# Filling TensorE's waits with f32 products, and eight row transfers for four, in a one-core decode block

## The chip, the cores and the metric

The kernel runs on one core of a Trainium2 chip. The time is the device time of one execution in microseconds (us). A profile is one execution of its own, recorded with every instruction and every DMA packet; its span runs from the first to the last instruction, and its own time is a little longer than the span.

## What is computed

One decode step for four sequences (B = 4, one token each, width D = 448), in f32: attention over a cache, and a pre-LayerNorm MLP behind it, both added to the row.

```python
B, Sq, D = 4, 1, 448
Hq, Hkv, Sk, Dh = 16, 8, 4096, 256
W = min(4096, max(256, Sk // 4))            # 1024: the last keys of the cache
q = (layernorm(x) @ wq).reshape(B, Sq, Hq, Dh).transpose(0, 2, 1, 3)
k, v = the last W of k_cache, v_cache       # two query heads share each of 8 kv heads
p = softmax(einsum("bhqd,bhkd->bhqk", q, k) * Dh ** -0.5)
h = x + einsum("bhqk,bhkd->bhqd", p, v).transpose(0, 2, 1, 3).reshape(B, Sq, Hq * Dh) @ wo
y = layernorm(layernorm(h))
return h + gelu(y @ w1 + b1) @ w2 + b2      # F = 1792
```

The keys and values of 8 groups are 64 MB, and with the weights the kernel reads some 88 MB once. Each matmul has few rows, since there are only four sequences and two heads to a group.

## The kernel before

**Groups.** The work goes over the 8 kv heads, called groups (`g`). Of each group the kernel needs: the part of wq (projection, L151), the keys (scores, L170), the softmax of 1024 scores (L182), the transposed probabilities `pT` (L202), the values (L215), and the part of wo (L233, L245), which adds into one PSUM tile `acc`.

**Loads.** The inputs are packed on the host so that a few large transfers bring them: `la`, `lb`, `lc`, `ld` (7 to 8 MB each, twice each) carry keys, values and weights in the order of use into a ring of three slots of SBUF (tiles `t`, `ta`, `tb`, `tc`, `td`, `te`; buffer numbers are left out in the profile). All of these are issued by SP (L57), in order; SP issues one when its slot is free. The last three slots are the `te`: e[0] has the keys of group 7 and w1, e[1] the values of group 6 and two parts of wo, e[2] the values of group 7 and w2, in pieces (L322 to L328; the last three pieces are 8, 4 and 2 parts of w2). Two small loads `wq_last` stand between the first keys and `ta` on SP's queue. ACT issues only the four transfers in question, the rows (L127): of each of the four quarters of a row, with 4 partitions of 704 numbers: x, b2 and b1 side by side, into tile `rs`, which POOL has cleared before. `rs` is read only at the end (`xb` in L386, `b2b` in L404, `b1b` in L429). Behind the row transfers ACT's queue has the table load and the copy of the first projection (L156).

**Engines.** TensorE's order is the order of the program text. The order on the other engines and the semaphores are set when the program is compiled. TensorE works on four column quadrants: a matmul of 32 output rows writes one quadrant, and four of them in a row go to four quadrants. An f32 matmul appears in the profile as two instructions.

**The last softmax.** For group 7 (`g + 1` with g = 6) the scores are followed by two matmuls on a bf16 tile of zeros, `idle`, into a PSUM tile that nobody reads (`warm0`), the transposes of p, ten more of the idle ones, and then the values of group 6, whose PSUM tile `po` takes the buffer of `warm0`:

```python
    keep_warm(2, warm0)
    transpose_p(g + 1, p)
    keep_warm(10, warm0)
    po = po_tile(g)
    values(g, vt, po)
```

Then come the values of group 7, the last parts of wo, the two LayerNorms, and the MLP: `pu` (w1, L416), `u` (gelu), `put`/`gT` (transposes), `pa` (the first 8 parts of w2, L449) with its copy `pas` on ACT (L453), `py` (the other 6 parts, L459, with `pas` added by L463), the result `res` (L465), and the output transfer.

Of the kernel before, what the change touches and what calls it, by code (L numbers as in the profile page):

```python
# [15 lines left out]
B, D = 4, 448  # L16
# [4 lines left out]
P = 128  # L21
# [4 lines left out]
FQ = F // 4  # L26
Q = 32
# [8 lines left out]
def block_kernel(ctx: ExitStack, tc, rows, wq0, k0, wq1, la, lb, lc, ld, k7, vo, w1, w2, out):  # L36
    nc = tc.nc
# [15 lines left out]
    def load(t, at, src, pieces=None):  # L53
        dst = t[:, at : at + src.shape[-1]]
        at = 0
        for n in pieces or (src.shape[-1],):
            nc.sync.dma_start(dst[:, at : at + n], src[:, at : at + n])  # L57
            at += n
        return dst

    def cut(t, sizes):
        parts, at = [], 0
        for n in sizes:
            parts.append(t[:, at : at + n])
            at += n
        return parts
# [11 lines left out]
    def keys(t):  # L78
        return t.rearrange("p (c b k) -> p c b k", c=2, b=B)
# [22 lines left out]
    yT = const.tile([P, ND + 1, Q], F32, name="yT")  # L102
# [21 lines left out]
    rs = const.tile([P, 2 * P + FQ], F32, name="rs")  # L124
    nc.gpsimd.memset(rs, 0.0)
    for j in range(4):
        nc.scalar.dma_start(rs[j * Q : j * Q + B, :], rows[j])  # L127
    xb, b2b, b1b = rs[:, :P], rs[:, P : 2 * P], rs[:, 2 * P :]


# [39 lines left out]
    def scores_half(g, h, kt):  # L170
        s = ps_s.tile([P, 512], F32, tag="s", name=f"s{g}_{h}")
        for c in range(2):
            for b in range(B):
                nc.tensor.matmul(  # L174
                    s[b * Q : (b + 1) * Q, :], qT[g % 2][:, c, b, :], kt[:, c, b, :],
                    start=(c == 0), stop=(c == 1),
                )
        m = work.tile([P, 1], F32, tag=f"mx{h}", name=f"mx{g}_{h}")
        nc.vector.reduce_max(m, s, axis=AX.X)  # L179
        return s, m  # L180

    def softmax(g, parts):  # L182
        halves, mx = zip(*parts)
        nm = work.tile([P, 1], F32, tag="nm", name=f"nm{g}")
        nc.vector.tensor_max(nm, mx[0], mx[1])
        nc.vector.tensor_scalar_mul(nm, nm, -SCALE)  # L186
        p = once.tile([P, 2 * 512], F32, tag="p", name=f"p{g}")
        sums = work.tile([P, 2], F32, tag="sums", name=f"sums{g}")
        for h in range(2):
            nc.scalar.activation(  # L190
                p[:, h * 512 : (h + 1) * 512], halves[h], AF.Exp, bias=nm, scale=SCALE,
                accum_out=sums[:, h : h + 1],
            )
        rec = work.tile([P, 1], F32, tag=f"rec{g % 3}", name=f"rec{g}")
        nc.vector.tensor_add(rec, sums[:, 0:1], sums[:, 1:2])
        nc.vector.reciprocal(rec, rec)
        return p, rec

    def scores(g, kt):
        return softmax(g, [scores_half(g, h, kt[h]) for h in range(2)])  # L200

    def transpose_p(g, p):  # L202
        for h in range(2):
            pt = ps_t.tile([P, 4, P], F32, tag="t", name=f"ppt{g}_{h}")
            for c in range(4):
                nc.tensor.transpose(pt[:, c, :], p[:, (4 * h + c) * P : (4 * h + c + 1) * P], ident)  # L206

            src = pt.rearrange("p (c i) (b q) -> p c i b q", i=2, b=B)
            for i in range(2):
                nc.vector.tensor_copy(  # L210
                    pT[g % 2][:, 2 * h : 2 * h + 2, :, i * REP : (i + 1) * REP], src[:, :, i, :, :REP]
                )
# [44 lines left out]
    def po_tile(g, pool=ps_o, tag="o"):  # L257
        return pool.tile([P, 2, DH], F32, tag=tag, name=f"po{g}")
# [22 lines left out]
    p, rec = scores(0, [keys(ka), keys(kb)])  # L281
# [7 lines left out]
    for g in (0, 3):  # L289
        ka, kb, wqt, va = cut(load(slot(f"ta{g}"), 0, la[g // 3]), (HALF, HALF, WEIGHTS, HALF))  # L290
        p, rec_next = scores(g + 1, [keys(ka), keys(kb)])
# [8 lines left out]
        p, rec_then = scores(g + 2, [keys(ka), keys(kb)])  # L300
# [11 lines left out]
        p, rec = softmax(g + 3, [first_half, scores_half(g + 3, 1, keys(kb))])  # L312
# [7 lines left out]
    g = HKV - 2  # L320
    e = [slot(f"te{i}") for i in range(3)]
    kt = [keys(t) for t in cut(load(e[0], 0, k7), (HALF, HALF))]  # L322
# [6 lines left out]
    p, rec_last = scores(g + 1, kt)  # L329


    warm0 = ps_o.tile([P, 512], F32, tag="o", name="warm0")

    def keep_warm(n, warm):
        for _ in range(n):
            nc.tensor.matmul(warm[:Q], idle[:, :Q], idle, start=True, stop=True)  # L336

    keep_warm(2, warm0)
    transpose_p(g + 1, p)
    keep_warm(10, warm0)  # L340
    po = po_tile(g)
    values(g, vt, po)
    po_last = po_tile(g + 1, ps_t, "t")
# [17 lines left out]
    for i in range(4):  # L361
        for j in range(4):
            nc.tensor.matmul(
                ph[j * Q : (j + 1) * Q], oT[(g + 1) % 2][:, i, :], columns(wo_last[:, i, :], j),
                start=False, stop=(i == 3),
# [3 lines left out]
    def w1_part(a, j):  # L369
        if a < 3:  # L370
            return slice(0, P), w1t[a][:, FQ * j : FQ * (j + 1)]
        rows = slice(H * (j // 2), H * (j // 2) + H)
        return rows, w1t[a][rows, FQ * (j % 2) : FQ * (j % 2 + 1)]
# [38 lines left out]
    for a in range(ND):  # L412
        m = Q if a == 0 else B
        for j in range(4):
            rows, w = w1_part(a, j)
# [31 lines left out]
    for c in range(first):  # L447
        j, m = c % 4, Q if c < 4 else B
# [6 lines left out]
    for c in range(first, NFC):  # L455
        for j in range(4):
            m, n = (Q, 2) if c == first else (B, 2 if j < 3 else 1)
# [80 lines left out]
```

## Time and profile before

| | |
|---|---|
| time, median of 3 runs | 215.27 us (214.98 to 215.72) |
| the profiled execution's own time | 214.81 us |
| its span | 213.0 us |
| mean granted TensorE clock in it | 0.848 |
| TensorE busy (matmul / weight load) | 137.4 us / 48.2 us |
| VectorE, ScalarE, GpSimd busy | 38.4, 21.2, 5.6 us |
| moved by DMA | 88.46 MB, mean 415 GB/s |

In the profile PE is TensorE, PEld its weight loads, DVE is VectorE, ACT is ScalarE, POOL is GpSimd and SP is SyncE; "SPq" and "ACTq" are their queues when they issue transfers. q1 is the DMA queue of SP, q10 that of ACT. Starts and lengths are in us from the span's start. A group of instructions is written as line, engine, operation, output<-input, shapes, count; brackets give the idle time before it and what ended it. For a transfer the last number is the median time from issue to landing.

### The profile page before, as it was taken

The numbers are of one execution on the slowest core, as the hardware profiler recorded it, in microseconds if no ns is written. First come the engines' busy times: TensorE is split into PE (matmuls) and PEld (weight loads), VectorE is DVE, ScalarE is ACT, GpSimd is POOL, SyncE is SP. The second block draws the span as 40 slices with busy tenths as digits, with TensorE's granted clock in tenths as the row PEclk, the third lists the DMA queues.
The fourth block names the chain that finished last, engine by engine and source line by source line (L and its number), as shares of the span: only waits on it lengthen the run. The fifth ranks groups of instructions, "written<-read, shape, count | busy, mean of one in ns | idle before, by whom it ended". The sixth has DMA issues, their size and how long they took to land.

```text
span 213.0 us, 2294 instructions
## 1 busy us (share of the span) xinstructions
PE 137.4 (64%) x971; PEld 48.2 (23%) x971; DVE 38.4 (18%) x167; ACT 21.2 (10%) x52; POOL 5.6 (3%) x17
## 2 busy tenths in 40 slices
PE   0456824872970595289398198239809876998993
PEld 0322211220220221023123022113202322334432
DVE  1420320320230012012114013100301223122320
ACT  0210110120020100021003001000000302000310
POOL 6100000000000000000000000000000000000110
PEclk9999995796697579769859959955965999999999
DMA  7999899999999999999999999999999998999990
GB/s 291 433 392 502 381 486 391 447 467 409 417 453 444 417 417 477 390 465 391 458 423 444 425 456 417 429 417 465 405 410 415 430 450 380 435 414 435 420 376 34
DMA packets 3289, 88.46 MB, mean 415 GB/s; under 512 B 384, under 2 KB 512, under 8 KB 1104
## 3 DMA queue, kind: packets, MB, share of 16 engines
q1 hardware_dynamic: 3248, 88.29, 96.7%
q8 instruction: 7, 0.11, 0.2%
q10 hardware_dynamic: 32, 0.05, 0.1%
q14 instruction: 2, 0.02, 0.0%
HBM read 88.26 MB, written 0.07 MB: 415 GB/s over the span
## 4 chain that ended last, share of the span: by engine, by line
DMA 64%; PE 29%; DVE 3%; ACT 1%; issue 1%; SPq 0%; ACTq 0%; DVEq 0%
DMA ta<-la 21%; DMA td<-ld 20%; DMA tb<-lb 16%; PE s L174 8%; DMA t<-k 8%; PE po L218 8%; PE ppt L206 2%; PE pu L416 2%; PE warm L336 1%; PE acc L247 1%; PE pq L154 1%; PE pot L239 1%; PE pa L449 1%; DVE o L235 1%; DVE mx L179 1%
## 5 line engine op out<-in xcount | busy, mean ns | idle before, releaser
L179 DVE TENSOR_REDUCE mx<-s 128x1 f32<-128x512 f32 x16 | 11.1, 691 | 61.0 <-PE s L174 61.0
L174 PE MATMUL s<-ta,qT 128*32 128x512 f32 x64 | 12.2, 935 | 8.9 <-DMA ta<-la 8.9
L156 ACT COPY qs<-pq 128x512 f32<-128x512 f32 x8 | 4.7, 585 | 112.3 <-PE pq L154 112.3
L190 ACT ACTIVATE p<-s,nm 128x512 f32<-128x512 f32 x16 | 10.9, 687 | 45.9 <-DVE nm L186 45.9
L174 PE MATMUL s<-td,qT 128*32 128x512 f32 x32 | 7.3, 1061 | 12.0 <-DMA td<-ld 12.0
L235 DVE TENSOR_SCALAR o<-po,rec 128x512 f32<-128x512 f32 x8 | 6.0, 751 | 47.1 <-PE po L218 47.1
L218 PE MATMUL po<-tb,pT 128*32 128x512 f32 x32 | 7.3, 1061 | 10.4 <-DMA tb<-lb 10.4
L154 PE MATMUL pq<-tc,yT 128*32 128x512 f32 (+1 forms) x20 | 3.9, 890 | 14.8 <-DMA tc<-lc 14.8
L206 PE MATMUL ppt<-ident,p 128*128 128x128 f32 x64 | 10.5, 286 | 2.0 <-ACT p L190 1.7
L218 PE MATMUL po<-tc,pT 128*32 128x512 f32 x64 | 10.5, 815 | 0.0
L160 PE MATMUL pqt<-ident,qs 128*128 128x128 f32 x32 | 6.6, 341 | 6.0 <-ACT qs L156 6.0
L174 PE MATMUL s<-tb,qT 128*32 128x512 f32 x64 | 9.1, 717 | 0.0
L206 PEld LDWEIGHTS ppt<-ident,p 128*128 128x128 f32 x64 | 6.7, 140 | 7.1 <-ACT p L190 7.1
L218 PE MATMUL po<-te,pT 128*32 128x512 f32 x64 | 7.9, 596 | 0.1
L162 DVE TENSOR_REDUCE sm<-pqt 128x16 f32<-128x64 f32 x8 | 1.8, 224 | 33.9 <-PE pqt L160 33.9
L174 PE MATMUL s<-t,qT 128*32 128x512 f32 x32 | 6.1, 925 | 2.6 <-DMA t<-k 2.6
L218 PE MATMUL po<-td,pT 128*32 128x512 f32 x64 | 7.3, 595 | 0.0
L336 PE MATMUL warm<-idle 128*32 128x512 bf16 x25 | 7.3, 382 | 0.0
L160 PEld LDWEIGHTS pqt<-ident,qs 128*128 128x128 f32 x32 | 4.2, 169 | 12.1 <-ACT qs L156 10.3
L174 PEld LDWEIGHTS s<-ta,qT 128*32 128x32 f32 x64 | 2.9, 163 | 17.4 <-issue 14.4
L239 PE MATMUL pot<-ident,o 128*128 128x128 f32 x32 | 5.2, 287 | 2.2 <-DVE o L235 2.2
L148 POOL TENSOR_TENSOR r<-ve_r,mhalf 128x1 f32<-128x1 f32 x2 | 1.1, 542 | 192.2 <-DVE ve_r L147 192.2
(129 smaller groups left out, 113.4 us busy)
## 6 DMA issues: line engine op xcount, KB each, us to landing
tc<-lc SPq DMA_DIRECT2D x2, 7936.0 KB
td<-ld SPq DMA_DIRECT2D x2, 7936.0 KB
ta<-la SPq DMA_DIRECT2D x2, 7040.0 KB, 29.4
tb<-lb SPq DMA_DIRECT2D x2, 7040.0 KB, 34.3
te<-vo SPq DMA_DIRECT2D x1, 4992.0 KB, 27.2
t<-k SPq DMA_DIRECT2D x1, 4864.0 KB, 16.4
te<-k SPq DMA_DIRECT2D x1, 4096.0 KB, 36.9
te<-w SPq DMA_DIRECT2D x2, 1792.0 KB, 28.0
```

The lines of the kernel that those rows point to most:

```text
L154: nc.tensor.matmul(pq[j * Q : (j + 1) * Q, cols], y, w, start=True, stop=True)
L156: nc.scalar.copy(qs, pq)
L160: nc.tensor.transpose(pt[:, i, :], qs[:, i * P : (i + 1) * P], ident)
L174: nc.tensor.matmul(s[b * Q : (b + 1) * Q, :], qT[g % 2][:, c, b, :], kt[:, c, b, :], start=(c == 0), stop=(c == 1),)
L179: nc.vector.reduce_max(m, s, axis=AX.X)
L190: nc.scalar.activation(p[:, h * 512 : (h + 1) * 512], halves[h], AF.Exp, bias=nm, scale=SCALE, accum_out=sums[:, h : h + 1],)
L206: nc.tensor.transpose(pt[:, c, :], p[:, (4 * h + c) * P : (4 * h + c + 1) * P], ident)
L218: nc.tensor.matmul(po[b * Q : (b + 1) * Q], pT[g % 2][:, c, b, :], vt[c][:, :, b, :], start=(c == 0), stop=(c == NKC // 2 - 1),)
L235: nc.vector.tensor_scalar_mul(o, po, rec)
L239: nc.tensor.transpose(pt[:, i, c], o[:, i, c * P : (c + 1) * P], ident)
L336: nc.tensor.matmul(warm[:Q], idle[:, :Q], idle, start=True, stop=True)
L416: nc.tensor.matmul(pu[j * Q : j * Q + m, :], zT[rows, a, :m], w, start=(a == 0), stop=(a == ND - 1),)
```

## The change

There are two edits. Around the last softmax, the twelve idle matmuls become three f32 products and two idle ones. A product multiplies yT with the first 512 columns of the last keys, which have landed by then; it writes the same unread tile. Two products stand ahead of the transposes of p, one product and the two idle matmuls behind them. And each of the four row transfers is split in two by columns: 256 numbers of x and b2, then 448 of b1, so that ACT issues eight.

```diff
     rs = const.tile([P, 2 * P + FQ], F32, name="rs")
     nc.gpsimd.memset(rs, 0.0)
     for j in range(4):
-        nc.scalar.dma_start(rs[j * Q : j * Q + B, :], rows[j])
+        parts = (slice(0, 2 * P), slice(2 * P, 2 * P + FQ))
+        for cols in parts:
+            nc.scalar.dma_start(rs[j * Q : j * Q + B, cols], rows[j][:, cols])
     xb, b2b, b1b = rs[:, :P], rs[:, P : 2 * P], rs[:, 2 * P :]
...
+    def fill(n):
+        for _ in range(n):
+            nc.tensor.matmul(warm0[:Q], yT[:, 0, :], kt[0][:, 0, 0, :], start=True, stop=True)
+
+    fill(2)
+    transpose_p(g + 1, p)
+    fill(1)
     keep_warm(2, warm0)
-    transpose_p(g + 1, p)
-    keep_warm(10, warm0)
     po = po_tile(g)
     values(g, vt, po)
```

## The prediction

> **What bounds the kernel now.** I read the page first, then the stages, then the waits of SP, the timeline of both ends, and the chain. The page's chain of what ended last:
>
> ```profile
> DMA 64%; PE 29%; DVE 3%; ACT 1%; issue 1%; SPq 0%; ACTq 0%; DVEq 0%
> ```
>
> Two thirds of the way to the end is transfers. The stages say how full they are (last two columns: DMA share of the 16 engines, GB/s; before them the granted TensorE clock):
>
> ```profile
> 2.00:206.00 204.00, 133.65 (x899) 46.44 (x899) 37.13 (x161) 20.35 (x49) 4.15 (x8) 0.84 1.00 430
> 207.00:208.00 1.00, 1.00 (x20) 0.30 (x16) 0.00 (x0) 0.00 (x0) 0.00 (x0) 1.00 0.60 240
> ```
>
> From 2 us to 206 the share is 1.00: the stream has no hole in which lost time could be made up, and it runs dry only within the last microseconds. A hole made anywhere arrives at the end whole. Two rows of the chain show the stream handing over to TensorE (start, length, what), here the first keys and the last ring slot:
>
> ```profile
> 1.18 16.36 DMA t<-k
> 117.86 42.28 DMA td<-ld
> 160.19 3.64 PE s L174 x16
> ```
>
> Keys 0 land at 17.54, ld's second load at 160.14, and TensorE starts on it at 160.19. From there it works without a DMA wait until the last weights. So two clocks meet at the end: TensorE's chain from 160.19, and the stream's last landing. Both edits touch one of them each.
>
> **Part one, the filling.** TensorE and ACT around the last softmax:
>
> ```profile
> 175.04 0.13 PEld L174 LDWEIGHTS s<-te,qT 128*32 128x32 f32 x4 [0.30 <-issue]
> 178.05 0.59 PE L336 MATMUL warm<-idle 128*32 128x512 bf16 x2
> 180.32 1.32 PE L206 MATMUL ppt<-ident,p 128*128 128x128 f32 x8 [1.68 <-ACT p L190]
> 181.57 2.33 PE L336 MATMUL warm<-idle 128*32 128x512 bf16 x10
> 183.96 0.16 PEld L218 LDWEIGHTS po<-te,pT 128*32 128x32 f32 x8 [0.55 <-PE warm L336]
> 183.97 4.50 PE L218 MATMUL po<-te,pT 128*32 128x512 f32 x40
> ```
>
> The ten idle ones behind the transposes are no filling of a wait: po's weight load waited 0.55 for them, nothing else. They cost 183.97 - 181.57 = 2.40 us on TensorE's chain. One idle matmul more costs (2.33 - 0.59)/8 = 0.217, and the last one of a group lasts 0.59 - 0.22 = 0.37.
>
> An f32 call makes two instructions (the eight calls of half the scores are the x16 above). The weight loads of a stage of full-length f32 products come in fours every 0.13 + 0.30 = 0.43 us, one for each column quadrant. The new products all write the same quadrant, which no row shows: between 0.11 each, if they overlapped as four quadrants do, and 0.43 each in series. I take 0.43, because the idle ones, which also share one quadrant, follow each other by their full 0.217.
>
> - Two products ahead of the transposes: 4 x 0.43 = 1.7, from 178.05 to 179.8. The transposes start at 180.32, when ACT has made p. Cost nothing; the cover is ACT and DVE's softmax, with 0.5 us to spare. Without that cover they would cost up to 1.7.
> - Behind the transposes: one product 0.86, one idle step 0.22, and the last one's 0.37: 181.57 + 1.45 = 183.02, against 183.90 before. The chain gains 0.88 (1.5 if the product overlapped, less than nothing only if TensorE ran at half clock, a rival below).
>
> Where that goes is read at the end:
>
> ```profile
> te<-vo SPq DMA_DIRECT2D x1, 4992.0 KB, 27.2
> 154.46 21.68 SPq L57 DMA_DIRECT2D te<-vo  x4
> te<-w SPq DMA_DIRECT2D x1, 896.0 KB, 26.1
> 207.83 0.64 PE L459 MATMUL py<-te,gT 128*32 128x128 f32 x16
> PEld py L459 <- DMA te<-w: 0.7, 1, 0.7
> 208.12 0.53 ACT L453 COPY pas<-pa 128x448 f32<-128x448 f32 x1 [1.56 <-PE pa L449]
> 208.70 0.43 PE L255 MATMUL py<-pas,sel 128*32 128x128 f32 x8 [0.23 <-ACT pas L453]
> 208.94 1.05 PE L459 MATMUL py<-te,gT 128*4 128x128 f32 x32
> ```
>
> vo's first load, issued at 154.46, lands 27.2 later at 181.7, ahead of the new 183.1, so values(6) is not held. The 896 KB of w2 are issued then (see the waits below) and land at 181.7 + 26.1 = 207.8: py starts at 207.83, right on the landing. A TensorE that comes 0.88 earlier waits there for the same landing. What remains is pas: its copy ends at 208.65, and adding its quadrants starts at 208.70. Earlier by 0.88, it no longer delays: sixteen py matmuls take about 0.45 (eight of the same shape and the step to the next take 0.24), so the next start is 208.28 and the gain 0.42. The last piece of w2, half as large (line 328), comes about 1.05 us behind at 430 GB/s, at 208.85, and is wanted at 208.28 + 0.24 + 0.45 = 208.97: just covered. **Part one is worth 0.4 us**, from 0 (covers gone) to 0.9 (if landings also moved).
>
> **Part two, eight transfers of the rows.** The four stand on ACT's queue; SP's at the same time, tb's load as the chain has it (issued, then 34.27 to landing), and what SP waited for (total, times, longest):
>
> ```profile
> 4.07 1.54 ACTq L127 DMA_DIRECT2D rs<-rows  x4
> 13.29 0.58 ACT L156 COPY qs<-pq 128x512 f32<-128x512 f32 x1 [6.37 <-PE pq L154]
> 1.63 1.55 SPq L267 DMA_DIRECT2D wq_last<-wq  x2
> 5.36 0.34 SPq L57 DMA_DIRECT2D ta<-la  x1
> 17.56 34.27 DMA tb<-lb
> SPq L57 <- DMA t<-wq: 2.2, 1, 2.2
> SPq L57 <- DMA t<-k: 11.9, 1, 11.9
> SPq L57 <- DMA te<-vo: 5.8, 2, 3.6
> ```
>
> Issuing four more costs ACT another 1.5 us at most, inside the 6.37 in which it waits for the first projection: nothing by itself. The waits are the point. ta waits for wq, and tb waits 11.9 us for the keys, to 17.56, though the third ring slot is still empty: neither needs the other's data. Count the transfers of SP and ACT together: wq, keys, four rows, two wq_last are eight; ta is the ninth and waited for the first, tb the tenth and waited for the second. At the end w2's last two pieces waited for vo: the 896 KB for its first load, eight before. So eight completion counters serve both queues in turn, and a transfer waits until the one eight before it has landed.
>
> With eight row transfers ta is the thirteenth and waits for the fifth. The kernel before hands the counters out in the order wq, keys, rows, wq_last. If that order stays, the fifth is the third row transfer; the two wq_last wait for the first and second row, ahead of ta on SP; the last row on ACT waits for the keys, and behind it stand ACT's table load and the copy of the first projection. When does the third row land? ACT's queue is q10; its packets in 8.8 to 11.5, 11.5 to 14.5, 14.5 to 16.3 and 16.3 to 17.5 (none earlier):
>
> ```profile
> q10 hardware_dynamic: 8, 0.01, 1.1%
> q10 hardware_dynamic: 8, 0.01, 1.0%
> q10 hardware_dynamic: 4, 0.01, 1.6%
> q10 hardware_dynamic: 12, 0.01, 2.8%
> ```
>
> Four transfers of four rows are 32 packets, eight each (four of data, four closing). They crawl between the large packets of the keys: the first is through by 11.5, the second by 14.5, the third only after 16.3, with the keys. Size does not set this pace, so halving the rows does not quicken it. ta is then issued not at 5.36 but at about 17.4 (17.6 if the keys themselves are what it waits for), with nothing behind the keys but crumbs. How long the engines stand still: the first bytes of the whole program, slices of 0.1 us from the start:
>
> ```profile
> DMA  0000000000000000099051046495593993996999
> 0.73 0.39 SPq L57 DMA_DIRECT2D t<-wq  x1
> t<-wq SPq DMA_DIRECT2D x1, 904.0 KB, 4.6
> t<-k SPq DMA_DIRECT2D x1, 4864.0 KB, 16.4
> ```
>
> Issued at 0.73, moving at 1.7: 1.0 from issue to bytes. ta moves from about 18.5. The engine that is last with the keys lost 18.5 - 17.54 = 1.0; the mean one, which at 430 GB/s is through with wq and keys (5.9 MB, 13.7 us from 1.7) and the small ones by about 16, loses 2.5. A load counts as landed with its last engine, and which one is last at the end may change, so the loss is an estimate between 1.0 and 2.5; I take 1.6, nearer the end that keeps the order of the engines. With no hole later it goes to the end whole, and 160.14 moves with 207.8, so part one stays worth 0.4.
>
> The Trainium skill, "DMA: Bandwidth & Descriptors", section Specifications, gives about 0.6 us to the first byte for transfers from SP or ACT; by it the loss would be 0.4 smaller and the sum 216.1. The row of this case says 1.0, and I keep it. The same page's Rules for kernel authors advise to coalesce small transfers, since under 64 KB one pays mostly overhead: the trace agrees with its 3 us from one row transfer (4 x 704 numbers) to the next.
>
> ACT's hold to 17.6 also delays what stands behind it:
>
> ```profile
> 17.68 6.06 PE L174 MATMUL s<-t,qT 128*32 128x512 f32 x32 [2.57 <-DMA t<-k]
> 24.64 0.33 SPq L57 DMA_DIRECT2D tc<-lc  x1
> ```
>
> Table load, copy, transposes and sums then follow the keys and move the first scores from 17.68 to about 21. That costs nothing: t's slot is handed to tc at 24.64 and would be at 28, while ta and tb keep the stream busy to 51.8 (17.56 + 34.27). Without that cover it would be 3.4.
>
> **Sum.** On the profiled execution, 214.81 with a span of 213.0: 214.81 + 1.6 - 0.4 = 216.0. It lay 0.46 under the median of 215.27, on which the forecast stands: 215.27 + 1.2 = 216.5.
>
> **Rivals.**
> 1. *ta is held longer*, 0.15. If seven rows stand ahead of the wq_last in the list, those wait for the keys, and ta for their issue (1.55): first bytes at 20.1, 1.5 later: 218.0. For it: the rows reach ACT late, behind a memset, at 4.07. Against it: wq_last's two issues came behind all four rows in the order of counters.
> 2. *ta is not held* (the other side: faster), 0.13. If the wq_last are listed ahead of the rows, or the added rows behind ta, ta waits for wq or for the first row, through by 11.5. It decides at about 15.5: issued before that, its bytes follow the keys without a hole. Then only the 0.4 is left: 214.9, and 214.4 if all of part one's 0.88 counts. Against it: the order of before, as above.
> 3. *The hole is small*, 0.1: the third row lands right behind its closing packets, which begin after 16.3. Issued at 16.6, ta moves at 17.6, a loss between 0.1 (last engine) and 1.6 (mean), say 0.6: 215.5.
> 4. *The filling overruns*, 0.04. At half clock (160 to 165 below, where sixteen score instructions take the 3.64 of the chain, 0.86 a round) 4 x 0.86 = 3.4 from 178.05 ends at 181.5, past 180.32: 1.2 late, the gain is gone, and the end is 0.3 late on top: 217.2. Against it:
>
> ```profile
> 160.00:165.00 5.00, 4.82 (x26) 1.35 (x26) 1.01 (x3) 0.00 (x0) 0.00 (x0) 0.50 0.97 416
> 178.00:180.00 2.00, 0.64 (x6) 0.10 (x1) 1.01 (x3) 0.51 (x1) 0.00 (x0) 1.00 1.04 444
> ```
>
> With TensorE busy 0.64 of 2 us the clock stayed at 1.00, and the change makes it busier there.
>
> **The numbers.** The forecast has 0.58, with its own range of 215.9 (loss 1.0) to 217.4 (loss 2.5). The range for 8 in 10 takes that, rival 3, the nearer part of rival 1 and the slower edge of rival 2: 214.9 to 217.8. A measurement of this kernel can tell 0.3%, 0.65 us, from no change: faster means under 214.6, slower over 215.9. Rival 2 centres just inside the first bound and reaches past it; I give 0.08 of its 0.13 to faster, since the 0.4 of part one can be up to 0.9. Its rest, rival 3 and a thin edge of the forecast are within: 0.2. The forecast's bulk and rivals 1 and 4 are slower: 0.72.
>
> **What would show it.** ta issued near 17.4 and not 5.36, with SP's wait before it on rows or keys; a hollow in the DMA share between 16.5 and 18.5; ld's second load landing near 161.7; ACT's first table load behind 17. At the end: fills done before p, values(6) about 0.9 us sooner after the transposes than the 2.40 of before, py again on the landing of w2 and no gap ahead of pas's quadrants. ta issued before 15 would make the prediction wrong in its sign.

## Result, and the profile after

The changed kernel takes 217.04 us (median of 6 executions, 216.85 to 217.24) against 215.5 for the kernel before in the same session (6 executions, 214.98 to 216.35): ratio 1.0071 (95% interval 1.0047 to 1.0094), slower by about 1.5 us. The profiled execution took 216.85 with a span of 215.1, at a mean granted clock of 0.849 (before: 214.81, 213.0 and 0.848). Lines of the changed kernel stand 2 further down than before's from line 129 on, and 7 further down behind the filling.

The start, in the timeline of after (start and length in us, queue or engine, line, operation):

```profile
4.07 13.50 ACTq L129 DMA_DIRECT2D rs<-rows  x8
10.77 3.78 SPq L269 DMA_DIRECT2D wq_last<-wq  x2
17.12 0.34 SPq L57 DMA_DIRECT2D ta<-la  x1
17.60 1.28 ACT L158 ACT_TABLE_LOAD   x1 [17.60 <-DMA rs<-rows]
21.31 5.36 PE L176 MATMUL s<-t,qT 128*32 128x512 f32 x32 [0.61 <-DVE qT L170]
27.59 0.33 SPq L57 DMA_DIRECT2D tc<-lc  x1
```

The eight row issues spread from 4.07 to 17.57, where four took 1.54. Behind them in the order of counters wq_last waits until 10.77 and ta until 17.12 instead of 5.36. What SP waited for (us in total, times, longest) names the rows, for wq_last and for the load of ta:

```profile
SPq L269 <- DMA rs<-rows: 11.4, 2, 9.2
SPq L57 <- DMA rs<-rows: 2.6, 1, 2.6
```

The hollow, in the stages (last two columns: DMA share and GB/s); first two rows from before, then two from after:

```profile
14.00:16.40 2.40, 1.08 (x4) 0.71 (x4) 0.48 (x3) 0.00 (x0) 0.00 (x0) 1.00 0.85 354
16.40:18.00 1.60, 0.32 (x4) 0.23 (x8) 0.00 (x0) 0.00 (x0) 0.00 (x0) 1.00 1.22 517
```

```profile
14.00:16.40 2.40, 0.00 (x0) 0.00 (x0) 0.00 (x0) 0.00 (x0) 0.00 (x0) 1.00 0.69 290
16.40:18.00 1.60, 0.00 (x0) 0.00 (x0) 0.00 (x0) 0.40 (x1) 0.00 (x0) 1.00 0.15 53
```

In these two stretches after has moved 64 x 2.4 + 464 x 1.6 = 896 thousand bytes less, or 0.9 MB (up to 14 us the two are level), which is 2.1 us at the mean rate of 430 GB/s. The chain of what ended last was 64% transfers and 29% TensorE; now the transfers have more of it, and it goes through the rows, then ta. The larger share comes with the filling and not with the rows: in the experiments below it is 79% with the filling alone and 63% with the rows alone. After's chain, and four pieces of it:

```profile
DMA 77%; PE 17%; POOL 1%; DVE 1%; ACT 1%; issue 1%; ACTq 0%; POOLq 0%
```

```profile
4.94 12.16 DMA rs<-rows
17.12 19.40 DMA ta<-la
48.43 43.24 DMA td<-ld
184.09 26.43 DMA te<-w
```

The end, in the timeline:

```profile
180.44 1.88 PE L342 MATMUL warm<-te,yT 128*32 128x512 f32 x4
182.72 1.32 PE L208 MATMUL ppt<-ident,p 128*128 128x128 f32 x8 [0.39 <-ACT p L192]
183.97 1.04 PE L342 MATMUL warm<-te,yT 128*32 128x512 f32 x2
184.85 0.59 PE L338 MATMUL warm<-idle 128*32 128x512 bf16 x2
185.51 4.50 PE L220 MATMUL po<-te,pT 128*32 128x512 f32 x40
210.56 0.64 PE L466 MATMUL py<-te,gT 128*32 128x128 f32 x16 [0.36 <-DMA te<-w]
210.94 0.48 PE L257 MATMUL py<-pas,sel 128*32 128x128 f32 x8
212.37 0.29 DVE L472 TENSOR_TENSOR res<-py,hb 128x128 f32<-128x128 f32 x1 [4.01 <-PE py L466]
```

From the end of the transposes to values(6) it is 185.51 - 183.97 = 1.54, against 2.40 before: 0.86 sooner. TensorE's gap ahead of the transposes is 0.39 instead of 1.68. The 896 KB of w2 land at 184.09 + 26.43 = 210.52, 2.7 later than before, py starts on that landing, and nothing waits ahead of pas's quadrants. The last sum starts at 212.37, before at 210.07: 2.30 later, which is 2.7 of the stream less 0.4 of the filling. The span grew by 2.1 only, because the last wait, for the output to land, was 0.9 instead of 1.2.

### The profile page after: what moved, and what is told of

Its sections match the earlier page's. It is cut to its first block, busy times and chain, and to the rows that moved or that the text cites. A ratio compares the mean times of both kernels' runs of the same rounds, so it can differ in the third digit from the quotient of the medians.

```text
span 215.1 us, 2293 instructions
## 1 busy us (share of the span) xinstructions
PE 137.2 (64%) x967; PEld 47.6 (22%) x967; DVE 38.4 (18%) x167; ACT 21.2 (10%) x52; POOL 5.6 (3%) x17
## 4 chain that ended last, share of the span: by engine, by line
DMA 77%; PE 17%; POOL 1%; DVE 1%; ACT 1%; issue 1%; ACTq 0%; POOLq 0%
DMA td<-ld 20%; DMA tc<-lc 17%; DMA te<-vo 13%; DMA te<-w 12%; DMA ta<-la 9%; DMA rs<-rows 6%; PE s L176 5%; PE po L220 5%; PE pq L156 2%; PE ppt L208 1%; PE pqt L162 1%; PE acc L249 1%; ACT qs L158 1%; PE py L466 1%; POOL pT L122 0%
## 5 line engine op out<-in xcount | busy, mean ns | idle before, releaser
L220 PE MATMUL po<-tb,pT 128*32 128x512 f32 x32 | 7.3, 1061 | 10.8 <-DMA tb<-lb 10.8
L162 PE MATMUL pqt<-ident,qs 128*128 128x128 f32 x32 | 6.6, 341 | 11.5 <-ACT qs L158 11.5
L212 DVE COPY pT<-ppt 128x16 f32<-128x16 f32 x32 | 4.7, 171 | 7.6 <-PE ppt L208 7.6
L176 PE MATMUL s<-t,qT 128*32 128x512 f32 x32 | 5.4, 833 | 0.6 <-DVE qT L170 0.6
```

The costliest lines, as they stand in the source:

```text
L162: nc.tensor.transpose(pt[:, i, :], qs[:, i * P : (i + 1) * P], ident)
L176: nc.tensor.matmul(s[b * Q : (b + 1) * Q, :], qT[g % 2][:, c, b, :], kt[:, c, b, :], start=(c == 0), stop=(c == 1),)
L212: nc.vector.tensor_copy(pT[g % 2][:, 2 * h : 2 * h + 2, :, i * REP : (i + 1) * REP], src[:, :, i, :, :REP])
L220: nc.tensor.matmul(po[b * Q : (b + 1) * Q], pT[g % 2][:, c, b, :], vt[c][:, :, b, :], start=(c == 0), stop=(c == NKC // 2 - 1),)
```

## Experiments

The medians below stand beside the kernel before, run on the same chip: 215.11 in the first group (22 executions), 215.22 in the second (34), 215.29 in the third (29).

**First group: which part costs, and through what.** The theory: eight completion counters serve the queues of SP and ACT in turn, and ta waits for the transfer eight ahead (1). Against it: the added transfers themselves slow the stream (2), or ACT, held by its own issues, comes late to its table load and copy (3).

*fill_only*: the filling, with four row transfers.

```diff
-        parts = (slice(0, 2 * P), slice(2 * P, 2 * P + FQ))
-        for cols in parts:
-            nc.scalar.dma_start(rs[j * Q : j * Q + B, cols], rows[j][:, cols])
+        nc.scalar.dma_start(rs[j * Q : j * Q + B, :], rows[j])
```

> The filling alone, with the four row transfers of before. Three theories on the row transfers agree here, since the rows are as before. ta is issued at 5.36. The values of group 6 start 0.86 to 0.88 sooner after the transposes, but py waits for the same landing of w2 at 207.8, so the end comes 0.4 us sooner than before (0.2%). If TensorE's chain alone were the bound it would be 0.9 us; if the products overran ACT's p, nothing or a loss.

214.48 (214.39 to 214.56), ratio 0.996 (0.9944 to 0.9977); profiled at 214.49, 0.32 under before's profiled execution.

```profile
181.90 26.01 DMA te<-w
207.95 0.64 PE L464 MATMUL py<-te,gT 128*32 128x128 f32 x16 [0.37 <-DMA te<-w]
```

The stream has not moved (landing at 207.91; before's py started at 207.83), and py waits for it. By medians the filling is worth 0.63, twice what the two profiles show; the second and third groups follow that.

*rows_only*: eight row transfers, with before's twelve idle ones.

```diff
-    fill(2)
     transpose_p(g + 1, p)
-    fill(1)
-    keep_warm(2, warm0)
+    keep_warm(10, warm0)
```

> The eight row transfers alone, with the tail of before. Theory 1 (counters: ta must wait for the third row, the stream runs dry behind the first keys): ta issued near 17.1, a hole of some 2 us in the DMA share between 16.4 and 18.4, and 2.0 to 2.7 us over before, 0.4 more than the whole change. Theory 2 (eight small transfers disturb the stream by themselves) and theory 3 (ACT, held by the last row, delays the first scores) give the same time here, theory 3 without needing the hole.

217.65 (216.66 to 218.37), ratio 1.0104 (1.0073 to 1.0135). The loss is all in the rows, and the filling takes part of it back. In its profile ta was issued at 16.62.

*five_rows*: as rows_only, but only the first row is split, so five transfers.

```diff
-        parts = (slice(0, 2 * P), slice(2 * P, 2 * P + FQ))
+        parts = (slice(0, 2 * P), slice(2 * P, 2 * P + FQ)) if j == 0 else (slice(0, 2 * P + FQ),)
```

> Only the first of the four row transfers is split, so five in all; tail of before. Theory 1: wq, keys, five rows and two wq_last are nine, ta is the tenth and waits for the second, the keys: issued at about 17.6, as dear as eight transfers or slightly dearer, 2.0 to 2.9 us over before; no row waits for the keys, so ACT is not held, its table load stays near 6 and the first scores near 17.7. Theory 2 (each small transfer costs its share): a quarter, about 0.5 us over. Theory 3 (ACT's hold costs): nothing, since ACT is free.

217.95 (217.69 to 218.98), ratio 1.0127 (1.0097 to 1.0156): no less than eight transfers cost.

```profile
5.98 1.28 ACT L158 ACT_TABLE_LOAD   x1 [5.98 <-issue]
17.39 0.34 SPq L57 DMA_DIRECT2D ta<-la  x1
```

```profile
SPq L57 <- DMA t<-k: 11.3, 1, 11.3
SPq L269 <- DMA t<-wq: 3.0, 1, 3.0
```

With five rows ta is the tenth transfer and waits for the second, the keys, as counting says. ACT is free at 5.98 here, so its hold is not what costs (against 3), and one transfer more costs as much as four more (against 2).

*wl_act*: the whole change, with wq_last's two loads issued by ACT ahead of the rows.

```diff
-        nc.sync.dma_start(
+        nc.scalar.dma_start(
```

> The whole change, but the two small wq_last loads are issued by ACT ahead of the rows instead of by SP ahead of ta. Then ta is the thirteenth still, but its fifth is the first row, and nothing stands ahead of it on SP: issued at about 10.8, before the keys are through at 16. ACT is still held to about 17.5 by the last row. Theory 1: no hole, and only the filling's 0.4 is left, so 0.4 us under before and 2 us under the whole change. Theory 2: as many small transfers, so 1.5 us over before. Theory 3: ACT held, first scores near 21, so 1.5 us over before.

215.54 (215.22 to 217.0), ratio 1.0021 (0.9998 to 1.0044). ta was expected at about 10.8 and came later, because the two 64 KB loads now stand ahead of the rows on ACT's queue (it moved 0.10 MB from 4 to 8 us and 0.03 MB from 8 to 11.5, which is these two), and SP's wait for the first row ended only then:

```profile
15.83 0.33 SPq L57 DMA_DIRECT2D ta<-la  x1
18.06 1.28 ACT L158 ACT_TABLE_LOAD   x1 [18.06 <-DMA t<-k]
```

The number missed; the cause stands. ACT is held longer than in after, yet the kernel is 1.5 us quicker: what counts is when ta is issued. Over the five profiles ta was issued at 5.4 (fill_only), 15.83, 16.62 (rows_only), 17.12 and 17.39, and the second load of w2 landed at 207.9, 209.05, 210.03, 210.52 and about 210.7. From 15.83 on, each tenth that ta comes later costs about a tenth; carried back to fill_only's landing, that line begins at about 14.6, which is an estimate, since no run issued ta between 5.4 and 15.83.

**Second group: counters of their own, and why the filling is worth more.**

*rows_pool*: the whole change, all eight rows still there, but issued by GpSimd.

```diff
-            nc.scalar.dma_start(rs[j * Q : j * Q + B, cols], rows[j][:, cols])
+            nc.gpsimd.dma_start(rs[j * Q : j * Q + B, cols], rows[j][:, cols])
```

> The whole change, but GpSimd issues the eight row transfers instead of ACT. Theory 1 (counters): its transfers have counters of their own, so SP issues ta and the rest without waiting for rows or keys, ACT isn't held, no hole: the same as the filling alone, 214.5, that is 0.6 under before and 2.5 under the whole change. Theory 2 (eight small transfers disturb the stream by themselves): as many small packets on the same engines, so about as slow as the whole change, 1.5 to 2 over before.

214.56 (214.35 to 214.81), ratio 0.9973 (0.996 to 0.9987): the loss is gone.

```profile
3.22 0.44 SPq L57 DMA_DIRECT2D ta<-la  x1
3.70 0.44 SPq L57 DMA_DIRECT2D tb<-lb  x1
9.98 4.27 POOL L129 DMA_DIRECT2D rs<-rows  x8
```

ta and tb wait for nothing, with the same eight small transfers in the stream, though issued later (9.98 to 14.25). With five_rows, this settles (1) against (2).

*direct*: before's rows, two products ahead of the transposes, nothing at all behind them.

```diff
     transpose_p(g + 1, p)
-    fill(1)
-    keep_warm(2, warm0)
```

> Four row transfers, two products ahead of the transposes, and nothing behind them: the values of group 6 follow at once. TensorE's chain is then 1.45 us ahead of the filling alone and 2.3 ahead of before. If the landing of w2 sets the end (my reading), this buys nothing more: 214.4 to 214.5, with as little scatter as the filling alone. If TensorE's chain still set it, 213.1. If the clock falls without the filling, slower.

214.47 (214.32 to 214.57), ratio 0.9957 (0.9942 to 0.9971), the same as fill_only.

```profile
181.93 4.50 PE L218 MATMUL po<-te,pT 128*32 128x512 f32 x40 [1.00 <-DMA te<-vo]
207.90 0.64 PE L462 MATMUL py<-te,gT 128*32 128x128 f32 x16 [0.27 <-DMA te<-w]
```

values(6) comes 1.37 sooner than fill_only's 183.30, and waits for vo and then for w2. The chain has no more to give; the landing sets the end.

*idle14*: before, with four idle ones more behind the transposes (`keep_warm(10, warm0)` to `keep_warm(14, warm0)`).

> Before with fourteen idle matmuls behind the transposes instead of ten, four row transfers: TensorE's chain is 4 x 0.217 = 0.87 us longer. My reading: in the faster executions of before the chain and the landing of w2 meet with no slack, in the slower ones the chain is already late because the clock came back later. Then nearly all of the 0.87 shows in both: 215.6 to 215.7 at the lowest, median near 216.0. If the landing alone set the end before, nothing shows.

215.78 (215.44 to 217.1), ratio 1.0047 (1.0026 to 1.0067), in two groups: seven executions from 215.44 to 215.79 and five from 216.32 to 217.1. The first lies about 1.0 above before's quicker executions (under 215); four times 0.217 is 0.87. The profile fell into the second, and its stages (TensorE clock third from the end) show what is different:

```profile
181.00:182.00 1.00, 1.00 (x6) 0.36 (x5) 0.32 (x3) 0.00 (x0) 0.00 (x0) 0.81 1.10 459
182.00:183.00 1.00, 1.00 (x4) 0.41 (x3) 0.00 (x0) 0.00 (x0) 0.00 (x0) 0.50 1.03 434
183.00:184.00 1.00, 1.00 (x4) 0.35 (x3) 0.00 (x0) 0.00 (x0) 0.00 (x0) 0.50 1.06 451
184.00:185.00 1.00, 1.00 (x3) 0.30 (x2) 0.00 (x0) 0.00 (x0) 0.00 (x0) 0.50 1.04 442
185.00:186.00 1.00, 1.00 (x5) 0.30 (x3) 0.00 (x0) 0.00 (x0) 0.00 (x0) 0.98 1.04 442
```

The clock loses 0.19 + 0.5 + 0.5 + 0.5 + 0.02 = 1.71 us, so it was halved for 3.42 us, from about 181.62 to 185.04, and that soon behind this gap, with only idle matmuls on TensorE:

```profile
179.93 1.32 PE L206 MATMUL ppt<-ident,p 128*128 128x128 f32 x8 [1.68 <-ACT p L190]
181.18 4.88 PE L336 MATMUL warm<-idle 128*32 128x512 bf16 x14
```

*last_piece*: fill_only, with the last 448 KB of w2 in two loads (`(8 * D, 4 * D, 2 * D)` to `(8 * D, 4 * D, D, D)`).

> The filling alone with w2 in pieces of 8, 4, 1 and 1 parts instead of 8, 4 and 2. The last landing stays where it is, near 209.0; behind it stand the matmuls of one part instead of two. If the last landing sets the end, 0.2 us less than the filling alone: 214.25. If the landing of the second piece does, or one more transfer costs as much, no change: 214.5 or a little more.

214.44 (214.23 to 214.52), ratio 0.9966 (0.9951 to 0.9981): no change against fill_only's 214.48. py still starts on the second load, at 207.80; the last one is not what is waited for.

**Third group: the gap and the clock.** Before's executions fall apart too: in the third session 13 lie from 214.5 to 214.96 and 16 from 215.2 to 216.11, in the first 11 from 214.56 to 214.91 and 11 from 215.31 to 216.17; in the second they spread over the same stretch without a clear break. Theory A: in the longer ones the 1.68 us gap has let the granted clock fall, so closing the gap alone should remove them, with ten idle ones kept behind.

*ahead_only*: before, with two products in place of the two idle ones ahead of the transposes.

```diff
-    keep_warm(2, warm0)
+    fill(2)
     transpose_p(g + 1, p)
     keep_warm(10, warm0)
```

> Before with the first two idle matmuls replaced by the two products ahead of the transposes; the ten idle ones behind stay, so does the four-transfer rows part. TensorE's chain is as long as before at full clock, but the gap of 1.68 us ahead of the transposes is closed. Theory A (the gap lets the clock fall to half in some executions, as the profiles of five rows and of fourteen idle ones show it, and that is the slower half of before's times): no execution near 215.5 or above, all between 214.6 and 214.9, median 214.8. Theory B (the slower half has another cause, and the filling gains only by shortening the chain): as scattered as before, median near 215.2.

214.58 (214.31 to 214.93), ratio 0.9962 (0.9943 to 0.9981): the longer group is gone.

```profile
179.70 1.32 PE L206 MATMUL ppt<-ident,p 128*128 128x128 f32 x8 [0.39 <-ACT p L190]
```

*two_idle*: before with the gap left open and two idle ones behind in place of ten.

> Before with two idle matmuls behind the transposes instead of ten and no products: the gap stays open, TensorE's chain is 8 x 0.217 = 1.74 us shorter at full clock. Theory A (the clock falls in some executions): those lose up to 1.7 us of the 3.4 us at half clock, about what the chain has gained, so the median is at the landing, 214.5, with a few executions a little above. Theory B (only the chain's length matters): 214.5 without exception.

214.45 (214.36 to 214.53), ratio 0.996 (0.9941 to 0.9978). A few longer executions were looked for and none came, but not because the clock held:

```profile
180.00:181.00 1.00, 1.00 (x5) 0.45 (x6) 0.59 (x6) 0.00 (x0) 0.00 (x0) 0.61 0.63 262
181.00:182.00 1.00, 0.85 (x6) 0.20 (x8) 0.01 (x1) 0.00 (x0) 0.00 (x0) 0.50 1.04 434
182.00:183.00 1.00, 1.00 (x8) 0.27 (x7) 0.00 (x0) 0.00 (x0) 0.00 (x0) 0.50 1.07 451
183.00:184.00 1.00, 1.00 (x8) 0.21 (x4) 0.00 (x0) 0.00 (x0) 0.00 (x0) 0.68 1.08 459
```

Again 0.39 + 0.5 + 0.5 + 0.32 = 1.71 of a halved clock, in an execution of 214.38. Without the eight idle ones TensorE's chain is 8 x 0.217 = 1.74 shorter, which covers the 1.71: py still waits for the landing of w2.

Of the five profiles with the gap of 1.68 (before, rows_only, five_rows, idle14, two_idle) three have a halved clock between 180 and 188; of the eight with 0.39 none has. No profile of before itself fell into its longer group, so for that kernel the cause rests on ahead_only and on the clocks that each execution lists: in the first group the 11 executions under 215 lie at 0.848 to 0.864 (mean 0.855), the 11 over it at 0.832 to 0.849 (mean 0.842), and the other two groups are alike. The clocks are the weaker evidence: the two ranges touch, and the longest executions list 0.849. wl_act also has three executions 0.65 and more above its other nine, with the gap closed; two of them list 0.865, as high as most of the nine, so a lower clock does not explain them, and no run does.

*pieces*: fill_only, with w2 in 8, 3, 2 and 1 parts, so that the second load is 672 KB.

```diff
-    w2t = cut(load(e[2], CACHE, w2, (8 * D, 4 * D, 2 * D)), NFC * (D,))
+    w2t = cut(load(e[2], CACHE, w2, (8 * D, 3 * D, 2 * D, D)), NFC * (D,))
```

> The filling alone with w2 in pieces of 8, 3, 2 and 1 parts instead of 8, 4 and 2. The filling alone waits for the second piece at 207.9; one part less in it lands about 0.5 us sooner, and the parts behind it land as TensorE comes to them. If that landing sets the end: 214.2, down to the last landing at 209.0 with one part behind it. If the end is set by the copy of pas (ready near 207.95) or by the last landing alone: no change, 214.45.

214.28 (214.15 to 214.41), ratio 0.9947 (0.9929 to 0.9965): the quickest version measured, under both kernels. Its profile shows the next wait:

```profile
207.51 0.64 PE L464 MATMUL py<-te,gT 128*32 128x128 f32 x16
208.35 0.42 PE L255 MATMUL py<-pas,sel 128*32 128x128 f32 x8 [0.21 <-ACT pas L458]
```

py no longer waits for the landing, and pas's copy is late again. That it beats fill_only by 0.2 rests on executions of two sessions; the two intervals overlap.

## Why the prediction was right, and where it was off

- **The counters, and ta held by them: right.** ta came at 17.12 where about 17.4 was forecast, SP waited for rows, and tb followed at 17.50. One added transfer does the same harm (five_rows), and the same transfers on GpSimd's queue do none (rows_pool). Rivals 1 and 2 fell with the order of the list, which stayed as the prediction had it. Rival 3's time for ta, 16.6, came in rows_only's profile (16.62), but w2 landed 2.1 later there than in fill_only's, not 0.6.
- **ACT's hold costs nothing: right.** The first scores moved to 21.31 and tc's load from 24.64 to 27.59, under the cover named. wl_act and five_rows show it from both sides.
- **The hole was sized at 1.6, the term that was off.** The engines' mean loss up to 18 us is 2.1; ta landed at 36.52, 1.76 late (before 34.76), ld's second load at 162.54, 2.4 late, and w2's second load 2.7 late. The choice of 1.6 leaned on the engines keeping their order at the end; nearer to the mean engine's 2.5 would have been right. That 2.5 in turn was too large by the first bytes of ta, which came at about 18.05 and not at 18.5. From the end of the issuing instruction they took 0.59 (18.05 - 17.46), and the program's first bytes 0.58 (1.7 - 1.12): the prediction's 1.0 counts the instruction itself, so its 1.0 and 0.6 do not contradict each other. The stream as a whole does not lose more on the way: from the start to 206 us it moved 422 GB/s against 426, which is 2.0 us. So single landings lie before or behind that mean; why that of w2 lies 0.7 behind it no run tells.
- **Part one's mechanism: right.** The chain gained 0.86 (forecast 0.88), py stayed on the landing, and 0.4 was left. direct shows that more on the chain brings nothing.
- **Part one's worth by the median was off.** The step that failed is the row under rival 4, from which it was read that the clock stays at 1.00 over the gap: one execution cannot say that. In about half of the kernel's executions something is lost there that the filling saves; ahead_only and the profiles beside it point to a clock halved behind the gap. So it is worth 0.63 by the median, not 0.4, while the profiled pair, both at full clock, shows 0.32 to 0.4.

The forecast of +1.2 met +1.5 by the medians partly because these two went in opposite directions: in the profiled pair alone the change is 216.85 - 214.81 = 2.04. And 215.5 is the median of only six executions of a kernel that falls in two groups: against the 215.11 to 215.29 of the larger groups the change would be 1.75 to 1.93. That the forecast came so near is partly luck; its mechanism is not.

The Trainium skill, "TensorE: Matmul & The Clock Gate", Part 1: The HAM clock gate, has a free-running window of about 3.4 us, after an idle one of which the clock is halved. The 3.42 us of both profiles agree with its length. A gap of 1.68 us, with two idle matmuls ahead of it and the transposes behind, was enough here, though, in some executions and not in others, so the window need not be idle throughout. In the three profiles the clock fell 1.0 to 1.7 us behind the gap's end, and the 3.42 us before the fall hold the whole gap. If that is the condition, a window at a chance place meets it in (3.42 - 1.68)/3.42 = 0.51 of executions. This is an estimate that no run tested; it fits the 27 longer ones of before's 51 in the first and third group.

## What to carry to other kernels

Before a transfer is added at the start, count those of SP's and ACT's queues together: here each waited for the one eight ahead of it, and a large load that ended up behind a slow small one left the stream empty. The order that counted, wq, keys, rows, wq_last, was neither that of the program text, which has the rows first, nor that of the issues in time, for in the kernel before wq_last was issued at 1.63 and the rows at 4.07; which transfer a load waits for is what shows it. Small loads that nobody needs soon can go to GpSimd's queue, whose transfers held up neither ta nor tb here; they took 7 to 29 us to land. Where the executions of a kernel fall in two groups, one profile shows only one of them: look for a gap on TensorE where the clock may fall, and fill it. Here two products did that; whether as many microseconds of idle matmuls would do was not run.

## What was not expected of the hardware

Two products of f32 (four instructions) and the end of the scores keep TensorE busy to 0.39 us ahead of the transposes, and the clock held there in all eight profiles; two idle bf16 ones and a gap of 1.68 let it be halved for 3.4 us in three of five. It is the gap that this shows, not the kind of matmul: in idle14 the clock came back to 1.00 at 185.04 with nothing but idle ones on TensorE since 181.25. And two loads of 64 KB put on ACT's queue ahead of the rows moved the landing of the first row from 10.77, when SP's wq_last was let go for it, to 15.83, when ta was: beside a 4.9 MB load, 128 KB ahead of it on its queue cost a row of 4 KB some 5 us.
